# A fused top-k attention and MLP kernel: which tiles VectorE turns, when the weights' second half is converted, and the order of some small steps

## The chip, the core and the metric

The kernel runs on one core of one Trainium2 chip. The metric is the device time of the one launch in microseconds (us). Before the change the median of three runs is 1632.91 us (1632.14 to 1634.82).

## The reference, cut to what matters

```
scores = 1/8 * q @ k^T                      # 8 batches, 8 heads, 576 x 576, head size 64, float32
keep the 32 largest of each row, softmax over them, attn @ v
x  = heads side by side                     # (8, 576, 512)
xn = (x - mean) / sqrt(var + 1e-6) * g_ln
out = x + relu(xn @ w_ch1) @ w_ch2          # 512 -> 2048 -> 512
```

q, k and v are float32. The weights and `g_ln` arrive as 64-bit floats, and the kernel makes 32-bit floats of them from their two 32-bit words.

## The kernel before, in words

**Units, groups, jobs.** A job is one batch and one pair of heads with two or three of the query tiles 0, 1, 2, 3 (128 rows) and 4 (the rest, 64 rows). A unit is one query tile of a job: for a whole tile two score tiles of 128 x 576, one per head; for the rest one tile that holds both heads. There are 68 jobs and 160 units. Batch 0 has the jobs [0,1], then [2,3], then [4], each for four pairs of heads; batch 1 has [0,1] and [2,3,4]; from batch 2 on it is [0,1,4] and [2,3].

**One loop, written out by hand.** `for n in range(END)` emits step n, and nothing is scheduled afterwards: on each engine the instructions run in the order of the code, and wait for each other by semaphores. Step n works on several units at once:

- TensorE makes the scores of unit n+2 (`scores`, L395) and ScalarE copies them out of PSUM (L376).
- VectorE finds the 32nd largest value of each row of unit n in four rounds (`select(u, 0..3)`, L438, L424, L430), and at the step's end takes the maximum and the minimum of the two halves of the next unit (`halve`, L416 and L417). The tile `hi` that `halve` writes has two buffers.
- For unit n-1 (`mk`): `watch` on GpSimd (L457) notes a difference of 2 columns, by which the kernel finds out at its end whether the shortened search was enough; `prepare` on ScalarE (L450, L451) scales threshold and maximum in place; `mask` is an activation on ScalarE (L486) and a subtraction on GpSimd (L489), and `weigh` the exponential on ScalarE (L497).
- For unit n-2 the weights `e` are turned, so that keys lie on partitions, into the tile `pt` (one buffer). This is done in one of two ways. Way one (`turn`): eight TensorE transposes through PSUM (L555) and two ScalarE copies of 128 x 512 (L567). Way two (`move`): two VectorE transposes of 32 x 32 blocks (L528) into the unit's own score tile `sc` (five buffers), then one DMA of 512 KB to HBM (L543), and in step n+3 of the unit four DMAs of 128 KB back into `pt` (L538, `bring`). The last 128 columns of both heads are turned on TensorE in both ways (L584, copied by L585). Way two is taken where `u.moved` is set.
- For a group whose last unit is `lag` steps back: `values` (attention times v, L609 and L616), `take_values` (L624), `place` (transpose L651, scale L628), which fills the rows x of the MLP. `lag` is 2 at first, 4 where the next job's first unit is moved, 3 elsewhere.

**The weights** come in 32 pieces, 16 of `w_ch1` and 16 of `w_ch2`. `batches` says which pieces are split in which step: four ahead of step 0, then 1 or 2 each step for steps 0 to 7 (`w_ch1`), 2 each in steps 8 to 15 (`w_ch2`). A piece is fetched by SP one step ahead (L147, into the pool `x`); `split` is three activations on ScalarE (L163, L164, L167) and, for `w_ch1`, a fourth that multiplies by `g_ln` (L169), and one clamp on GpSimd (L170); `shift` is one VectorE instruction (L173) a step later; `join` is two GpSimd instructions (L179, L181). In steps below `LAZY` = 7 the joins stand at the step's end, later in its middle. `CONVERTING` is the last step with pieces, plus 2.

**The MLP** runs in 18 blocks of 256 rows. `give` adds a block's matmuls to `todo` when its rows are placed; `fill`, called about eight times a step, takes from it as many as the step's `share` allows. The share is even over the steps up to the next block. The first block (`gives_first`, step 9) is the only one whose rows are handed over within the step (`quick`).

**SP** issues all DMAs (ScalarE those of the first two jobs' q), in the order of the code.

The function `compute` with its loop, `split`, `prepare`, `watch`, `settle_watch`, `tell` and `turn` are those that the change touches.

Of the kernel before, what the change touches and what calls it, by code (L numbers as in the profile page):

```python
# [10 lines left out]
ALU = mybir.AluOpType  # L11
# [8 lines left out]
STEEP = 2.0**90  # L20
# [9 lines left out]
def compute(  # L30
# [12 lines left out]
    nc = tc.nc  # L43
    P = nc.NUM_PARTITIONS
# [46 lines left out]
    def const(shape, name):  # L91
        return consts.tile(shape, FP32, tag=name, name=name)
# [5 lines left out]
    def turned():  # L98
        return brief("tp")
# [5 lines left out]
    ends = const([P, P], "ends")  # L105
    nc.gpsimd.memset(ends[:], 0.0)
    if doubt is not None:
        watched = const([P, 34], "watched")
        nc.gpsimd.memset(watched[:], -1.0)
    ident = const([P, P], "ident")  # L110
    make_identity(nc, ident[:])
# [10 lines left out]
    class Piece:  # L122
# [26 lines left out]
        def split(self):  # L149
            i = self.i  # L150
            high = self.raw[:, :, 1].bitcast(FP32)
            if i < NF:
                self.size = hpool.tile([P, DM], U32, tag="h", name="size")[:]
                self.low = wt_rows[:, i % 8]
                homes = ((opool, "o"), (opool, "o"), (rpool, "r"), (rpool, "r"), (xtpool, "xT"))
            else:
                self.size = wt_rows[:, 2 * i % 8].bitcast(U32)
                self.low = wt_rows[:, (2 * i + 1) % 8]
                homes = ((opool, "o"), (opool, "o"), (rpool, "r"))
            pl, tag = homes[i % len(homes)]  # L160
            self.sign = pl.tile([P, DM], FP32, tag=tag, name="sign")
            size_f = self.size.bitcast(FP32)
            nc.scalar.activation(size_f, high, AF.Abs)  # L163
            nc.scalar.activation(  # L164
                self.low, self.raw[:, :, 0], AF.Copy, bias=2.0, scale=2.0**-51
            )
            nc.scalar.activation(self.sign[:], high, AF.Sign)  # L167
            if self.i < NF:
                nc.scalar.mul(self.sign[:], self.sign[:], gcol[:, self.c : self.c + 1])  # L169
            nc.gpsimd.tensor_scalar(size_f, size_f, HIGH_MAX, HIGH_MIN, ALU.min, ALU.max)  # L170

        def shift(self):
            nc.vector.tensor_scalar(  # L173
# [22 lines left out]

    batches = {}
    queue = list(pieces)
    for n in range(-1, NF):
        count = 4 if n < 0 else 1 + (n + 1) % 2 if n < NF // 2 else 2  # L200
        batches[n], queue = queue[:count], queue[count:]
    assert not queue

# [2 lines left out]
    def weights(n, phase):  # L206

        now, before = batches.get(n, []), batches.get(n - 1, [])  # L210
        if phase == 0:
            for x in batches.get(n + 1, []):
                x.fetch()
            for x in now[0::2]:
                x.split()
        elif phase == 1:
            for x in before:
                x.join()
            for x in now[1::2]:
                x.split()  # L220
# [149 lines left out]
    def scores(u):  # L370

        u.sc = scpool.tile([P, 2, S], FP32, tag="sc", name="sc")
        made = [score_half(u, s) for s in range(2)]
        for t in range(len(u.tiles)):
            for s in range(2):
                nc.scalar.copy(  # L376
                    u.sc[:, t, s * HALF : (s + 1) * HALF], made[s][t][:, 0:HALF]
                )
# [67 lines left out]
    def prepare(u):  # L446

        nt = len(u.tiles)
        u.bias, u.edge = u.top[:, 0:nt, 0], u.thr[:, 0:nt, 7]
        nc.scalar.mul(u.edge, u.edge, STEEP)  # L450
        nc.scalar.mul(u.bias, u.bias, -scale)  # L451

    def watch(u):

        nt = len(u.tiles)
        c = 1 + 2 * (u.i % 16)
        nc.gpsimd.tensor_tensor(  # L457
            watched[:, c : c + nt], u.hi[:, 0:nt, HALF + 7], u.thr[:, 0:nt, 7], ALU.subtract
        )
        if u.i % 16 == 15 or u.i == N - 1:  # L460
            u.ends_watch = True

    def settle_watch():

        for out, first, op in ((0, 0, ALU.max), (33, 1, ALU.min)):
            nc.vector.tensor_reduce(
                watched[:, out : out + 1], watched[:, first : first + 33],
                mybir.AxisListType.X, op,
            )

    def tell():

        w = hpool.tile([P, J * P], FP32, tag="h", name="tell")
        nc.gpsimd.memset(w[:], 0.0)
        nc.vector.tensor_scalar(w[:, 1:2], watched[:, 33:34], -1.0e38, None, ALU.is_le)
        nc.vector.tensor_scalar(w[:, 0:1], watched[:, 0:1], 0.0, None, ALU.is_ge)
        nc.vector.tensor_tensor(w[:, 0:1], w[:, 0:1], w[:, 1:2], ALU.max)
        ps = brief("tell")
        nc.tensor.transpose(ps[:, 0:P], w[:, 0:P], ident[:])
        nc.vector.tensor_reduce(w[0:1, P : P + 1], ps[0:1, 0:P], mybir.AxisListType.X, ALU.max)  # L480
        nc.vector.tensor_copy(doubt, w[0:1, P : P + 1])
# [64 lines left out]
    def turn(u):  # L546

        g = u.group
        i0 = place_of(u)
        q0 = i0 * 32  # L550

        def part(t):
            ps = turned()
            for c in range(J):
                nc.tensor.transpose(  # L555
                    ps[:, c * P : (c + 1) * P], u.e[:, t, c * P + t * R : (c + 1) * P + t * R],
                    ident[:],
                )
            if u.rest:
                both = ps[:].rearrange("p (c h n) -> p h c n", h=2, n=R)  # L560
                for h in range(2):
                    nc.scalar.copy(
                        g.blocks[:, h, i0 : i0 + R // 32],
                        both[:, h].rearrange("p c (i n) -> p i c n", n=32),
                    )
            else:
                nc.scalar.copy(  # L567
                    g.blocks[:, t, i0 : i0 + P // 32],
                    ps[:].rearrange("p (c i n) -> p i c n", c=J, n=32),
                )  # L570

        def last():
            ps = turned()
            if u.rest:
                nc.tensor.transpose(ps[0:R, 0:P], u.e[:, 0, JP:S], ident[:])
                nc.tensor.transpose(ps[:, P : 2 * P], u.e[:, 0, JP - R : S], ident[:])
                for h in range(2):
                    nc.scalar.copy(
                        g.pt[h * R : (h + 1) * R, 2 * J, q0 : q0 + R],
                        ps[h * R : (h + 1) * R, h * (P + R) : h * (P + R) + R],  # L580
                    )
            else:
                ends = u.e[:].rearrange("p t n -> p (t n)")[:, JP : JP + P]
                nc.tensor.transpose(ps[:, 0:P], ends, ident[:])  # L584
                nc.scalar.copy(g.pt[:, 2 * J, q0 : q0 + P], ps[:, 0:P])  # L585

        heads = () if u.moved else range(len(u.tiles))
        return [lambda t=t: part(t) for t in heads] + [last]

    xs, xps, rs, oTr, dr = {}, {}, {}, {}, {}  # L590

# [30 lines left out]
    def take_values(g):  # L622
        g.oT = otpool.tile([P, GQ], FP32, tag="oT", name="oT")
        nc.scalar.copy(g.oT[:, 0 : g.nq], g.av[:, 0 : g.nq])  # L624
# [405 lines left out]
    CONVERTING = max(n for n in batches if batches[n]) + 2  # L1030
    EARLY = jobs[NHP].first

    for u in units[jobs[5 * NHP].first :]:
        u.moved = not u.rest and u is not u.group.units[-1]


    for j, after_j in zip(jobs, jobs[1:] + [None]):
# [43 lines left out]
    def at(i):  # L1081
        return units[i] if 0 <= i < N else None
# [10 lines left out]
    def due(n):  # L1093

        return units[n + 2 : n + 3]
# [87 lines left out]
    for n in range(END):  # L1185
# [15 lines left out]

        moved = ex is not None and ex.moved

        if n:
            for x in due(n):
                scores(x)
        if g:
            values(g)
        if n in brings:
            brings.pop(n)()  # L1210
            turn(at(n - 3))[-1]()
        if quick:
            take_values(g)
        if u:
            select(u, 0)
        if quick:
# [8 lines left out]
        if n in keeps:  # L1225
            keep_heads(keeps[n])
        if doubt is not None and at(n - 2) and at(n - 2).ends_watch:
            settle_watch()
            if n == N + 1:
                tell()  # L1230
        if mk and doubt is not None:
            watch(mk)
        if early:
            prepare(ex)
            for t in range(2):
                mask(ex, t)
            if n < gives_first - 1:
                weights(n, 0)
            for t in range(2):
                weigh(ex, t)  # L1240
        if not early or n == gives_first - 1:
            weights(n, 0)
        fill()
        if mk and not early:
# [4 lines left out]
            mask(mk, 1)  # L1249
        if g and not quick:  # L1250
            take_values(g)
        if parts:
            parts[0]()
        if ex and ex.rest:
# [25 lines left out]
        fill()  # L1280
        if n in ends_due:
            fill_ends(ends_due.pop(n))
        if g and not quick:
            place(g)
        if late:
            place_rest(late.job.b, late.job.hp)
        fill(1 if g or late else 0)
        if mk and mk.i >= EARLY:
            weigh(mk, 0)
        fill()  # L1290
        if len(parts) > 2:
            parts[1]()
# [20 lines left out]
        fill()  # L1313
        if u:
            select(u, 3)
        if nxt:
            halve(nxt)
        if n < LAZY:
# [76 lines left out]
```

## Time and profile before

| what | value |
|---|---|
| runs, median of three | 1632.91 us |
| the profiled execution's own time | 1631.76 us |
| its span | 1629.8 us |
| granted TensorE clock, mean | 0.969 |
| TensorE busy | 1499.9 us |
| VectorE busy | 1348.7 us |
| ScalarE busy | 1108.6 us |
| GpSimd busy | 1029.1 us |
| DMA traffic | 211.49 MB, 45.2% of 16 engines' span on SP's queue |
| VectorE transposes of `e` (L528) | 144 instructions for 72 units |
| TensorE transposes of `e` (L555) | 576 instructions |
| last unit's `halve` starts | 1468.2 us after the start |

Line numbers are those of the kernel before. PE is TensorE, PEld its weight loads, DVE VectorE, ACT ScalarE, POOL GpSimd; a "q" behind a name is that engine's queue. Busy time is the union of an engine's instructions. An engine is idle before an instruction while it waits for another engine; the profile names the one that came last. A step of the loop is read on VectorE, from one `halve` (L416) to the next.

### The profile page before, as it was taken

To read this page: it belongs to the slowest core of one execution; us is meant where nothing else is said; L and a number is where in the kernel's file an instruction comes from. 1 tells how busy PE (TensorE), PEld (TensorE's weight loads), DVE (VectorE), ACT (ScalarE), POOL (GpSimd) and SP (SyncE) were. 2 spreads that over 40 slices of the span, in tenths; PEclk is the share of its full clock that TensorE was granted. 3 is DMA by queue.
4 is the path that set the end of the run, shared out by engine and by line. 5 is a ranking of instruction groups with operands and counts; after the bars stand their busy time and mean duration, and the time that the engine had idled before them with its cause. 6 is when DMAs were issued, how large, how long until landed. Compare 5 with 4: busy or idle time off the path is not lost.

```text
span 1629.8 us, 27190 instructions
## 1 busy us (share of the span) xinstructions
PE 1499.9 (92%) x7898; PEld 1131.1 (69%) x7898; DVE 1348.7 (83%) x3939; ACT 1108.6 (68%) x3032; POOL 1029.1 (63%) x1473
## 2 busy tenths in 40 slices
PE   2556889899999999999999999999999999999997
PEld 1334646577767677777777777777777777778886
DVE  6866679698999999999999998998899999992000
ACT  6885767678777676777666867677667776764311
POOL 4775875865666676767765747465657666656344
PEclk9867899999999999999999999999999999999999
DMA  8432335312365456545564465546554455432211
GB/s 216 134 99 82 111 80 118 118 57 68 85 167 180 120 148 166 162 145 142 152 189 133 137 152 172 163 116 175 146 171 149 127 155 159 155 98 85 66 39 54
DMA packets 355685, 211.49 MB, mean 130 GB/s; under 512 B 247492, under 2 KB 327880, under 8 KB 355528
## 3 DMA queue, kind: packets, MB, share of 16 engines
q1 hardware_dynamic: 350792, 209.08, 45.2%
q8 instruction: 65, 1.06, 0.3%
q10 hardware_dynamic: 4736, 0.59, 0.2%
q14 instruction: 92, 0.75, 0.2%
HBM read 145.62 MB, written 63.96 MB: 129 GB/s over the span
## 4 chain that ended last, share of the span: by engine, by line
PE 64%; POOL 15%; ACT 12%; DVE 7%; issue 1%; DMA 1%; ACTq 0%; SPq 0%; POOLq 0%; DVEq 0%
PE hps L754 23%; PE ops L911 19%; PE scps L395 8%; POOL e L489 6%; PE av L609 5%; ACT e L486 3%; PE tp L555 3%; DVE m L438 2%; DVE hi L424 2%; PE av L616 2%; ACT sc L376 2%; POOL h L847 1%; ACT e L497 1%; POOL w L181 1%; PE xo L651 1%
## 5 line engine op out<-in xcount | busy, mean ns | idle before, releaser
L489 POOL TENSOR_TENSOR e<-e,sc 128x576 f32<-128x576 f32 x288 | 423.1, 1486 | 441.1 <-ACT e L486 434.0
L754 PE MATMUL hps<-xT,w 128*128 128x256 f32 x2304 | 546.2, 384 | 7.3 <-ACT xT L716 7.3
L754 PEld LDWEIGHTS hps<-xT,w 128*128 128x128 f32 x2304 | 425.0, 192 | 74.1 <-issue 11.5
L438 DVE MAX8 m<-hi 128x8 f32<-128x296 f32 (+1 forms) x1152 | 471.2, 444 | 0.2
L424 DVE MATCH_REPLACE8 hi<-m,hi 128x288 f32<-128x288 f32 (+1 forms) x864 | 377.7, 442 | 0.0
L911 PE MATMUL ops<-w,h 128*128 128x256 f32 x1360 | 322.3, 383 | 1.4 <-POOL h L847 1.4
L911 PEld LDWEIGHTS ops<-w,h 128*128 128x128 f32 x1360 | 251.3, 192 | 40.1 <-issue 5.8
L376 ACT COPY sc<-scps 128x288 f32<-128x288 f32 x576 | 199.1, 407 | 99.3 <-PE scps L395 77.7
L497 ACT ACTIVATE e<-e,m 128x576 f32<-128x576 f32 x288 | 224.8, 781 | 59.5 <-POOL e L489 58.0
L486 ACT ACTIVATE e<-sc,m 128x576 f32<-128x576 f32 x288 | 212.4, 769 | 0.0
L416 DVE TENSOR_TENSOR hi<-sc 128x576 f32<-128x576 f32 (+1 forms) x160 | 135.4, 846 | 59.7 <-POOL watched L457 55.3
L609 PE MATMUL av<-pt,vb 128*64 128x256 f32 (+2 forms) x1088 | 147.2, 412 | 5.9 <-ACT pt L567 4.8
L417 DVE TENSOR_TENSOR lo<-sc 128x576 f32<-128x576 f32 (+1 forms) x160 | 144.1, 901 | 0.0
L555 PE MATMUL tp<-ident,e 128*128 128x128 f32 x576 | 94.0, 291 | 47.0 <-ACT e L497 47.0
L395 PE MATMUL scps<-kT,late_qT 64*128 64x288 f32 (+3 forms) x832 | 129.2, 419 | 8.6 <-ACT pt L567 6.0
L777 ACT ACTIVATE h<-hps 128x512 f32<-128x512 f32 x144 | 85.2, 592 | 66.7 <-PE hps L754 65.7
L911 PE MATMUL ops<-wt,s 128*128 128x256 f32 x544 | 129.3, 381 | 0.0
L555 PEld LDWEIGHTS tp<-ident,e 128*128 128x128 f32 x576 | 76.8, 150 | 69.7 <-ACT e L497 52.3
L528 DVE STREAM_TRANSPOSE sc<-e 128x512 f32<-128x512 f32 x144 | 94.3, 687 | 33.4 <-POOL h L847 16.7
L609 PEld LDWEIGHTS av<-pt,vb 128*64 128x64 f32 x1088 | 72.8, 141 | 67.2 <-issue 15.5
L430 DVE MAX8 hi<-lo 128x8 f32<-128x288 f32 x288 | 117.7, 444 | 0.0
L395 PEld LDWEIGHTS scps<-kT,late_qT 64*128 64x128 f32 (+1 forms) x832 | 72.3, 171 | 61.8 <-issue 18.7
(104 smaller groups left out, 1887.4 us busy)
## 6 DMA issues: line engine op xcount, KB each, us to landing
turned<-sc SPq DMA_DIRECT2D x72, 512.0 KB, 2.9
pt<-turned SPq DMA_DIRECT2D x288, 128.0 KB, 2.7
w<-forms SPq DMA_DIRECT2D x136, 256.0 KB, 3.9
vb<-in_v_dram SPq DMA_DIRECT2D x68, 288.0 KB, 3.9
raw<-in_moe_w_ch_dram SPq DMA_DIRECT2D x32, 512.0 KB, 3.5
kT<-kept SPq DMA_DIRECT2D x36, 288.0 KB, 3.5
kin<-in_k_dram SPq DMA_DIRECT2D x128, 72.0 KB, 2.8
kept<-kT SPq DMA_DIRECT2D x32, 288.0 KB, 3.0
```

The lines of the kernel that those rows point to most:

```text
L376: nc.scalar.copy(u.sc[:, t, s * HALF : (s + 1) * HALF], made[s][t][:, 0:HALF])
L395: nc.tensor.matmul(ps[i * R : i * R + ql, o : o + width], qT[r, q0 : q0 + ql], kT[r, k0 : k0 + width], start=True, stop=True,)
L417: nc.vector.tensor_tensor(lo, a, b, ALU.min)
L424: nc.vector.match_replace(x, m[:, t, :], x, LOWEST)
L438: nc.vector.max(m[:, t, :], u.hi[:, t, 0:width])
L486: nc.scalar.activation(u.e[:, t], u.sc[:, t], AF.Relu, bias=u.edge[:, t : t + 1], scale=-STEEP)
L489: nc.gpsimd.tensor_tensor(u.e[:, t], u.e[:, t], u.sc[:, t], ALU.subtract)
L497: nc.scalar.activation(u.e[:, t], u.e[:, t], AF.Exp, bias=u.bias[:, t : t + 1], scale=-scale, accum_out=g.den[:, col : col + 1],)
L555: nc.tensor.transpose(ps[:, c * P : (c + 1) * P], u.e[:, t, c * P + t * R : (c + 1) * P + t * R], ident[:],)
L609: nc.tensor.matmul(av[h * D : (h + 1) * D, 0 : g.nq], vb[:, h * (J + 1) + c, :], g.blocks[:, h, 0 : g.nq // 32, c, :], start=(c == 0), sto ...
L754: nc.tensor.matmul(ps[0][:, side * N : (side + 1) * N], w1[:, c, f * P : (f + 1) * P], self.xT[:, c, 0:N], start=(c == 0), stop=(c == NC - 1),
L911: nc.tensor.matmul(bank[name][:, 0:Q], a(j), rhs, start=first and j == 0, stop=(j == G - 1), skip_group_check=not first,)
```

## The change

- **More units are moved.** `u.moved` was set from batch 2 on for whole tiles that are not the last of their group. It is now set from unit 8 (`EARLY`) on for every whole tile that is not its job's last, and for a job's last one too where the next job begins with a whole tile. In the built program VectorE has 236 transposes of `e` where it had 144, TensorE 368 transposes of `e` (heads and ends together) where it had 736, ScalarE 20 copies of 128 x 512 where it had 112, and SP 118 and 472 DMAs for the moves where it had 72 and 288. So 118 units are moved where 72 were; of the 46 new ones 7 are moved in steps 10 to 16, 15 in steps 22 to 39, 23 in steps 40 to 158 and 1 in step 159.
- **The weights' second half pauses.** Steps 8 and 9 split nothing; `w_ch2` is split in steps 10 to 17. `CONVERTING` becomes 19.
- **The factor g_ln** is multiplied on GpSimd (16 instructions of 128 x 512) and no longer on ScalarE; the clamp is emitted ahead of it.
- **The note** `watch` is emitted at the end of its unit's own step, and not at the start of the next. Its store is doubled, and `prepare` writes the scaled threshold to another column, so that it need not wait for the note.
- **Order.** Up to step 9 `values` (and at step 9 `take_values`) come ahead of `scores`. The ends of a moved unit are transposed where they were, but copied later, after the masks. `place` and `place_rest` come after a fill and the first `weigh`. At step 8 the weights stand between the masks and `weigh` as in the steps before it.

```diff
             nc.scalar.activation(size_f, high, AF.Abs)
+            nc.gpsimd.tensor_scalar(size_f, size_f, HIGH_MAX, HIGH_MIN, ALU.min, ALU.max)
...
             nc.scalar.activation(self.sign[:], high, AF.Sign)
             if self.i < NF:
-                nc.scalar.mul(self.sign[:], self.sign[:], gcol[:, self.c : self.c + 1])
-            nc.gpsimd.tensor_scalar(size_f, size_f, HIGH_MAX, HIGH_MIN, ALU.min, ALU.max)
+                nc.gpsimd.tensor_scalar(
+                    self.sign[:], self.sign[:], gcol[:, self.c : self.c + 1], 1.0,
+                    ALU.mult, ALU.mult,
+                )
...
-    for n in range(-1, NF):
-        count = 4 if n < 0 else 1 + (n + 1) % 2 if n < NF // 2 else 2
+    for n in range(-1, NF + 2):
+        count = 4 if n < 0 else 1 + (n + 1) % 2 if n < NF // 2 else 0 if n < NF // 2 + 2 else 2
...
-        u.bias, u.edge = u.top[:, 0:nt, 0], u.thr[:, 0:nt, 7]
-        nc.scalar.mul(u.edge, u.edge, STEEP)
+        u.bias, u.edge = u.top[:, 0:nt, 0], u.thr[:, 0:nt, 6]
+        nc.scalar.mul(u.edge, u.thr[:, 0:nt, 7], STEEP)
...
-    for u in units[jobs[5 * NHP].first :]:
-        u.moved = not u.rest and u is not u.group.units[-1]
+    for j, nj in zip(jobs, jobs[1:] + [None]):
+        for u in units[max(j.first, EARLY) : j.last + 1]:
+            u.moved = not u.rest and (
+                u.i < j.last or nj is not None and not units[nj.first].rest
+            )
...
-        if n:
-            for x in due(n):
-                scores(x)
-        if g:
+        late_ends = None
+        ahead = due(n) if n else []
+        if g and n <= gives_first:
+            values(g)
+        if quick:
+            take_values(g)
+        for x in ahead:
+            scores(x)
+        if g and n > gives_first:
             values(g)
         if n in brings:
             brings.pop(n)()
-            turn(at(n - 3))[-1]()
-        if quick:
-            take_values(g)
+            late_ends = turn_ends(at(n - 3))
...
-        if mk and doubt is not None:
-            watch(mk)
...
+        if late_ends:
+            late_ends()
...
+        fill(1 if g or late else 0)
+        if mk and mk.i >= EARLY:
+            weigh(mk, 0)
         if g and not quick:
             place(g)
         if late:
             place_rest(late.job.b, late.job.hp)
-        fill(1 if g or late else 0)
-        if mk and mk.i >= EARLY:
-            weigh(mk, 0)
...
         if u:
             select(u, 3)
+            if doubt is not None:
+                watch(u)
```

`turn_ends` is the former last part of `turn`, with the transposes and the copy separated; `watched`, `settle_watch` and `tell` follow the doubled store.

More of the change, by code (lines that the diff above doesn't have):

```diff
@@ L107, in compute @@
     if doubt is not None:
-        watched = const([P, 34], "watched")
+        watched = const([P, 2, 34], "watched")
         nc.gpsimd.memset(watched[:], -1.0)
@@ L455, in watch @@
         nt = len(u.tiles)
-        c = 1 + 2 * (u.i % 16)
+        half, c = u.i // 16 % 2, 1 + 2 * (u.i % 16)
         nc.gpsimd.tensor_tensor(
-            watched[:, c : c + nt], u.hi[:, 0:nt, HALF + 7], u.thr[:, 0:nt, 7], ALU.subtract
+            watched[:, half, c : c + nt], u.hi[:, 0:nt, HALF + 7], u.thr[:, 0:nt, 7], ALU.subtract
         )
@@ L461, in watch, with settle_watch @@
             u.ends_watch = True
-    def settle_watch():
+            u.half = half
+    def settle_watch(half):
         for out, first, op in ((0, 0, ALU.max), (33, 1, ALU.min)):
             nc.vector.tensor_reduce(
-                watched[:, out : out + 1], watched[:, first : first + 33],
+                watched[:, half, out : out + 1], watched[:, half, first : first + 33],
                 mybir.AxisListType.X, op,
@@ L474, in tell @@
         nc.gpsimd.memset(w[:], 0.0)
-        nc.vector.tensor_scalar(w[:, 1:2], watched[:, 33:34], -1.0e38, None, ALU.is_le)
-        nc.vector.tensor_scalar(w[:, 0:1], watched[:, 0:1], 0.0, None, ALU.is_ge)
-        nc.vector.tensor_tensor(w[:, 0:1], w[:, 0:1], w[:, 1:2], ALU.max)
+        nc.vector.tensor_scalar(w[:, 2:4], watched[:, :, 33], -1.0e38, None, ALU.is_le)
+        nc.vector.tensor_scalar(w[:, 4:6], watched[:, :, 0], 0.0, None, ALU.is_ge)
+        nc.vector.tensor_reduce(w[:, 0:1], w[:, 2:6], mybir.AxisListType.X, ALU.max)
         ps = brief("tell")
@@ L572, in last, with turn_ends, copy @@
         def last():
-            ps = turned()
+            turn_ends(u)()
+        heads = () if u.moved else range(len(u.tiles))
+        return [lambda t=t: part(t) for t in heads] + [last]
+    def turn_ends(u):
+        q0 = place_of(u) * 32
+        g = u.group
+        ps = turned()
+        if u.rest:
+            nc.tensor.transpose(ps[0:R, 0:P], u.e[:, 0, JP:S], ident[:])
+            nc.tensor.transpose(ps[:, P : 2 * P], u.e[:, 0, JP - R : S], ident[:])
+        else:
+            ends_e = u.e[:].rearrange("p t n -> p (t n)")[:, JP : JP + P]
+            nc.tensor.transpose(ps[:, 0:P], ends_e, ident[:])
+        def copy():
             if u.rest:
-                nc.tensor.transpose(ps[0:R, 0:P], u.e[:, 0, JP:S], ident[:])
-                nc.tensor.transpose(ps[:, P : 2 * P], u.e[:, 0, JP - R : S], ident[:])
                 for h in range(2):
@@ L582, in last @@
             else:
-                ends = u.e[:].rearrange("p t n -> p (t n)")[:, JP : JP + P]
-                nc.tensor.transpose(ps[:, 0:P], ends, ident[:])
                 nc.scalar.copy(g.pt[:, 2 * J, q0 : q0 + P], ps[:, 0:P])
-        heads = () if u.moved else range(len(u.tiles))
-        return [lambda t=t: part(t) for t in heads] + [last]
+        return copy
     xs, xps, rs, oTr, dr = {}, {}, {}, {}, {}
@@ L1227, in compute @@
         if doubt is not None and at(n - 2) and at(n - 2).ends_watch:
-            settle_watch()
+            settle_watch(at(n - 2).half)
             if n == N + 1:
                 tell()
-        if mk and doubt is not None:
-            watch(mk)
         if early:
@@ L1236, in compute @@
                 mask(ex, t)
-            if n < gives_first - 1:
-                weights(n, 0)
+            weights(n, 0)
             for t in range(2):
                 weigh(ex, t)
-        if not early or n == gives_first - 1:
+        if not early:
             weights(n, 0)
```

## The prediction

> **What bounds the kernel now.** I read the busy time in five stretches first, cut at the starts of VectorE's steps 9, 19 (235 us), 40 and 159; columns: stretch, length, busy time and instructions of PE, PEld, DVE, ACT, POOL, granted clock, DMA share, GB/s.
>
> ```profile
> 0.00:111.00 111.00, 50.57 (x212) 31.63 (x212) 83.16 (x247) 89.12 (x206) 73.48 (x83) 0.86 0.58 157
> 111.00:235.00 124.00, 94.04 (x410) 61.20 (x411) 81.70 (x239) 88.02 (x218) 88.78 (x91) 0.82 0.31 95
> 235.00:418.00 183.00, 174.99 (x982) 123.57 (x983) 152.84 (x481) 135.91 (x388) 115.97 (x166) 0.97 0.33 86
> 418.00:1468.00 1050.00, 1028.19 (x5553) 783.78 (x5550) 1018.61 (x2934) 752.30 (x2121) 676.52 (x997) 1.00 0.53 149
> 1468.00:1630.00 162.00, 152.07 (x745) 130.91 (x743) 12.41 (x40) 43.27 (x102) 74.34 (x137) 0.99 0.20 61
> ```
>
> No engine fills the first two stretches: steps there hang on chains between engines. In the third TensorE is at 96% and VectorE at 84%. In the fourth both are at 97 to 98%. The fifth is the last blocks' matmuls; VectorE has next to nothing left. Up to 1468 VectorE is idle for 27.8 + 42.3 + 30.2 + 31.4 = 131.7 us. Where, the waits of VectorE and ScalarE tell (total us, times, longest):
>
> ```profile
> DVE hi L416 <- POOL watched L457: 55.3, 27, 7.1
> DVE wt L173 <- POOL wt L170: 28.8, 6, 8.4
> ACT pt L585 <- PE tp L584: 76.2, 50, 4.5
> ACT m L450 <- POOL watched L457: 54.8, 35, 5.1
> ACT sign L167 <- POOL w L181: 18.1, 5, 4.8
> ```
>
> The first is VectorE's `halve` waiting for its buffer until GpSimd has noted; 10.5 us of it lie in the first stretch, 2.9 in the second, 24.7 in the third, 17.2 in the fourth. The second lies in steps 11 to 16, where the weights' second half is converted. Then the prices, from the groups (busy us, mean ns, idle before):
>
> ```profile
> L528 DVE STREAM_TRANSPOSE sc<-e 128x512 f32<-128x512 f32 x144 | 94.3, 687 | 33.4 <-POOL h L847 16.7 <-ACT e L497 16.1 <-POOL e L489 0.6
> L555 PE MATMUL tp<-ident,e 128*128 128x128 f32 x576 | 94.0, 291 | 47.0 <-ACT e L497 47.0
> L567 ACT COPY pt<-tp 128x512 f32<-128x512 f32 x112 | 65.4, 584 | 17.2 <-PE tp L555 16.7
> L169 ACT ACTIVATE sign<-sign,gcol 128x512 f32<-128x512 f32 x16 | 11.6, 722 | 0.5
> L170 POOL TENSOR_SCALAR size<-size 128x512 f32<-128x512 f32 x16 | 11.2, 698 | 19.8 <-ACT size L163 19.8
> ```
>
> Last, step 9 in order of time (start, duration, idle before): scores go ahead of the first block's values, and VectorE waits for the rows.
>
> ```profile
> 117.28 2.46 PE L395 MATMUL scps<-kT,late_qT 64*128 64x288 f32 x6
> 120.57 1.33 PE L395 MATMUL scps<-kT,late_qT 64*128 64x288 f32 x2 [0.83 <-ACT pt L567]
> 121.82 3.68 PE L609 MATMUL av<-pt,vb 128*64 128x256 f32 x16
> 128.04 0.70 DVE L679 BATCH_NORM_STATS2 st<-x 128x6 f32<-128x512 f32 x1 [9.35 <-ACT x L628]
> ```
>
> **One more moved unit** costs VectorE two L528 at 94.3/144 = 0.655 us: 1.31 us. It saves TensorE eight L555 at 94.0/576 = 0.163 us: 1.3 us, and ScalarE two L567: 1.17 us. SP issues five DMAs more. For 46 units: 60.3 us more on VectorE, 60.1 less on TensorE, 53.7 less on ScalarE, 47 MB more traffic. What counts is where VectorE has room. The Trainium skill (VectorE: DVE Perf Modes, "Rules for kernel authors") speaks against this: a 128 x 128 transpose belongs on TensorE if PSUM will do as its destination. By that rule alone the 60.3 us would be a plain loss, an estimate of 1693 us; the rows above disagree so far as VectorE idles beside a TensorE at 96%.
>
> **Stretch 1, to step 8: -7 us.** From step 3 on ScalarE sets the pace: its L450 starts at 45.7 us and, six steps later, at 111.1, so 10.9 us a step, while VectorE has 8.1 to 9.5 of work. ScalarE loses L169: seven pieces in steps 3 to 8, 7 x 0.72 = 5.1 us. At the start L450 waits 5.07 us for a note that stands behind eight joins; these still stand before the subtraction, so I count 2 of it. The new 16 factors on GpSimd cost about what the clamp costs undisturbed, 0.615 us, 9.8 in all; GpSimd waits 1.6 to 3.2 us a step for masks there, and that covers them. If it doesn't, they delay the note and the subtraction: +5. If all of `halve`'s waits go: -10.5.
>
> **Stretch 2, steps 9 to 18: -11 us.** Values ahead of scores bring the rows earlier by 121.82 - 117.28 = 4.5 us, and step 8 starts 1.5 us sooner without `halve`'s wait: -6. VectorE's wait of 9.35 us covers no more than that. The pause moves eight steps of pieces by two, with all their instructions and 16 fetches; it removes none, so its value is only that ScalarE and GpSimd enter them without arrears. In steps 12 to 15 (52.3 us, 13.1 each) the loop is: first join, sign of the next piece, exponentials, copies, next split, masks, subtraction, join; VectorE waits about 4.4 us a step beside it, so seven moves at 1.31 (9.2 us) are covered there, and ScalarE's loop loses one or two L567 each. I take -5 for these, between -29 (all 28.8 us of L173's wait gone) and +9 (the moves paid in full). Later weights delay the first block's second product by two steps; TensorE has room for it (76% busy).
>
> **Stretch 3, steps 19 to 39: -3 us.** 15 moves: VectorE 152.8 + 19.7 = 172.5; TensorE 175 - 19.5 = 155.5. So VectorE becomes the bound here. Of its 30.2 us of waits, steps 25 to 27 hold 12.9, where the note stood behind four form-making instructions of 1.27 us; it is now ahead of them. I leave 7.5: 180 instead of 183. Ends: 172.5 (-11) and 202.7 (+20, no wait shrinks).
>
> **Stretch 4, steps 40 to 158: +12 us.** 23 moves: VectorE 1018.6 + 30.1 = 1048.7, which is the whole stretch of before. TensorE falls to 998. Its relief ends some of VectorE's 31.4 us of waits, and ScalarE gets free of L585 (65.8 us here, for the copy now stands behind the masks) and of L450's 31.7. But `watch` keeps its place on GpSimd behind the same subtractions. I leave 13 of 31.4: 1062. Ends: 1049 (-1) and 1080 (+30).
>
> **Queues.** On SP each new unit puts a send behind the fetches, which wait for ScalarE (L147 behind L167: 103.1 us in 21 waits, 4.9 each), and four reads that wait for `values` to free `pt` (L538 behind L616: 195.2 us in 41). Behind the send waits only the score buffer's next use, in the step after; a 512 KB send lands in 2.9 us. A group's last unit now arrives one step ahead of its values, not two: 1.7 us of issue and 2.8 of landing in a step of 8.7. No time counted; without that cover one landing, about 4.5 us, a group in the weights' steps. The copy `late_ends` and `place` only move behind work of their own engine.
>
> **Tail: 0.** The work behind the last unit is the same but for one moved unit; its VectorE time lies beside 152 us of TensorE.
>
> **Sum:** -7 - 11 - 3 + 12 = -9 on a span of 1629.8: 1620.8. Around the span lie 1631.76 - 1629.8 = 2.0 us, and the median is 1.15 above that run: 1624.
>
> On the port: with L179 at 134.07 us taking 1.77 us, its usual 1.27, VectorE's L417 took 1.81 instead of 0.75. The Trainium skill (SBUF — State Buffer, "Who interferes with whom") says a VectorE instruction with two SBUF inputs and a GpSimd one exclude each other for a whole instruction; by it the factors could hold VectorE for up to 16 x 0.615 = 9.8 us, an estimate, and the sum would be 1634. I keep 1624: the factors run in the first stretch alone, where VectorE isn't the bound.
>
> **Rivals.**
> - *VectorE pays in full from step 19 on* (slower side). Its 38 new moves cost 49.8 us, and its waits there, 30.2 + 31.4, stay because GpSimd's queue and not TensorE ends them: with stretches 1 and 2 at -18 that is +32, 1665; with 18 us of waits gone 1647. For it: 41.9 of the 61.6 us are the wait for the note, behind GpSimd. Against: GpSimd itself waits 434 us for ScalarE's masks, and ScalarE is relieved. It decides when over 45 x 1.31 = 59 of the 131.7 us of idle can't be filled, that is, when more than 72.7 remain.
> - *The weights' steps run at VectorE's pace.* 81.7 + 9.2 = 90.9 us of work, about 8 of waiting in step 9 and 4 elsewhere: stretch 2 takes 103 and not 113, so 1614. For it: ScalarE's copies leave the loop. Against: GpSimd alone has 10 us a step.
> - *SP is late.* The send held by 4.9 us and passed on to ScalarE's copies in the seven units of stretch 2: up to +34, more likely a quarter of it, which takes the gain away: 1633. For it: L147's waits. Against: ScalarE waited only 4.0 us for sends so far.
> - That it doesn't do what it says: 118 units and not 117 are moved, which changes nothing; and where no joins or forms lie between, the note keeps its place.
>
> **Chances.** Forecast, 1614 to 1633: 0.46, of which 0.08 lie within 0.2%. Weights' steps: 0.19. SP: 0.08, half within, half slower. VectorE in full: 0.27. A measurement here can tell 0.2%, 3.3 us. Faster 0.38 + 0.19 = 0.57; same 0.08 + 0.04 = 0.12; slower 0.04 + 0.27 = 0.31. The forecast's own range, 1612 to 1634, lets each stretch miss by a fifth of its bounds; the range that leaves out no more than 2 in 10 runs from 1602, below the second case, to 1648, the first rival's middle.
>
> **What would show it.** Stretch 4 on VectorE at 1049 us or more busy and under 15 idle; L416's wait for the note under 25 in all; L173's wait still about 20; step 9 at 17 us; L450's wait near none; TensorE idle in the fourth stretch. If VectorE's idle time before the last unit stays over 80 us, the forecast is wrong; if it falls under 55, the second rival is right.

## The result, and the profile after

The changed kernel takes 1661.6 us (median of four runs, 1657.9 to 1663.9) against 1633.6 us for the kernel before in the same session (1632.1 to 1634.8): a ratio of 1.017, 95% interval 1.0149 to 1.0191. The forecast said 1624 us, and slower at most 1648. The profiled execution has a span of 1660.4 us, 30.6 more than before.

Line numbers of the changed kernel differ a little: `halve` is now L419 (maximum) and L420 (minimum), VectorE's transposition of `e` is L532, the note is L460, the factor is L170 on GpSimd.

First the five stretches, cut again at the starts of VectorE's steps 9, 19, 40 and 159. Columns as before: stretch, length, busy time and instructions of PE, PEld, DVE, ACT, POOL, granted clock, DMA share, GB/s.

```profile
0.00:116.00 116.00, 53.83 (x212) 33.78 (x212) 88.51 (x247) 79.10 (x193) 91.19 (x98) 0.81 0.54 145
116.00:243.00 127.00, 95.22 (x383) 58.53 (x385) 93.74 (x253) 82.58 (x207) 86.14 (x89) 0.84 0.52 154
243.00:434.00 191.00, 164.05 (x860) 118.91 (x858) 183.83 (x511) 123.22 (x362) 130.26 (x174) 0.92 0.55 158
434.00:1497.00 1063.00, 1017.56 (x5334) 770.63 (x5331) 1055.81 (x2982) 715.58 (x2063) 694.20 (x993) 0.98 0.59 171
1497.00:1660.00 163.00, 153.64 (x749) 132.25 (x747) 13.63 (x41) 43.50 (x102) 74.35 (x137) 0.99 0.22 68
```

From one cut to the next the kernel is 5, 3, 8, 13 and 2 us longer. VectorE is now the fullest engine of the third and the fourth stretch (96% and 99%), and TensorE has room there. Then the groups of VectorE that matter (busy us, mean ns, idle before), and the factor's group:

```profile
L420 DVE TENSOR_TENSOR lo<-sc 128x576 f32<-128x576 f32 (+1 forms) x160 | 169.7, 1060 | 0.0
L532 DVE STREAM_TRANSPOSE sc<-e 128x512 f32<-128x512 f32 x236 | 153.2, 685 | 28.6 <-POOL h L863 14.1 <-ACT e L501 8.8 <-POOL s L857 5.8
L419 DVE TENSOR_TENSOR hi<-sc 128x576 f32<-128x576 f32 (+1 forms) x160 | 144.3, 902 | 11.7 <-POOL watched L460 7.5 <-ACT sc L379 4.2
L170 POOL TENSOR_SCALAR sign<-sign,gcol 128x512 f32<-128x512 f32 x16 | 14.0, 873 | 2.5 <-ACT sign L168 1.4
```

In the kernel before, the two halving lines were these:

```profile
L417 DVE TENSOR_TENSOR lo<-sc 128x576 f32<-128x576 f32 (+1 forms) x160 | 144.1, 901 | 0.0
L416 DVE TENSOR_TENSOR hi<-sc 128x576 f32<-128x576 f32 (+1 forms) x160 | 135.4, 846 | 59.7 <-POOL watched L457 55.3 <-ACT sc L376 4.1
```

The wait for the note fell from 55.3 to 7.5 us, as hoped. But the same 320 instructions became 34.5 us longer (279.5 to 314.0). The other waits of before are gone or moved (total us, times, longest):

```profile
ACT e L501 <- POOL e L493: 126.8, 141, 7.2
ACT sc L379 <- DMA turned<-sc: 87.2, 33, 5.6
...
ACT pt L597 <- PE tp L589: 6.6, 10, 1.2
```

and in the kernel before:

```profile
ACT e L497 <- POOL e L489: 58.0, 97, 2.3
ACT sc L376 <- DMA turned<-sc: 4.0, 3, 2.1
```

ScalarE no longer waits for the ends (76.2 us before, 6.6 now) nor for the note; it waits for GpSimd's masks instead (58.0 before, 126.8 now) and for the sends of transposed tiles (4.0 before, 87.2 now). Last, the chain that ended last, of the changed kernel and of the kernel before: VectorE has 30% of it (7% before), transfers 6% (1% before).

```profile
PE 47%; DVE 30%; POOL 9%; ACT 7%; DMA 6%; issue 2%; SPq 0%; ACTq 0%; POOLq 0%; DVEq 0%
PE 64%; POOL 15%; ACT 12%; DVE 7%; issue 1%; DMA 1%; ACTq 0%; SPq 0%; POOLq 0%; DVEq 0%
```

### The profile page after: what moved, and what is told of

The parts are those of the page before. It is cut to its first block, busy times and chain, and to the rows that moved or that the text cites. A ratio compares the mean times of both kernels' runs of the same rounds, so it can differ in the third digit from the quotient of the medians.

```text
span 1660.4 us, 26850 instructions
## 1 busy us (share of the span) xinstructions
PE 1484.3 (89%) x7530; PEld 1114.1 (67%) x7530; DVE 1435.5 (86%) x4031; ACT 1044.0 (63%) x2924; POOL 1076.1 (65%) x1489
## 2 busy tenths in 40 slices
DMA packets 388807, 259.74 MB, mean 156 GB/s; under 512 B 251172, under 2 KB 355112, under 8 KB 388648
## 4 chain that ended last, share of the span: by engine, by line
PE 47%; DVE 30%; POOL 9%; ACT 7%; DMA 6%; issue 2%; SPq 0%; ACTq 0%; POOLq 0%; DVEq 0%
PE hps L770 17%; PE ops L927 15%; DVE m L441 9%; DVE hi L427 7%; PE scps L398 6%; PE av L625 4%; DVE sc L532 4%; DMA turned<-sc 3%; POOL e L493 3%; DVE lo L420 3%; DVE hi L419 3%; DVE hi L433 2%; DMA pt<-turned 2%; ACT sc L379 1%; PE av L632 1%
## 5 line engine op out<-in xcount | busy, mean ns | idle before, releaser
L770 PE MATMUL hps<-xT,w 128*128 128x256 f32 x2304 | 535.8, 385 | 0.7 <-ACT xT L732 0.7
L770 PEld LDWEIGHTS hps<-xT,w 128*128 128x128 f32 x2304 | 434.9, 194 | 65.0 <-issue 7.0
L441 DVE MAX8 m<-hi 128x8 f32<-128x296 f32 (+1 forms) x1152 | 470.0, 443 | 0.1
L379 ACT COPY sc<-scps 128x288 f32<-128x288 f32 x576 | 196.6, 408 | 197.6 <-DMA turned<-sc 87.2
L501 ACT ACTIVATE e<-e,m 128x576 f32<-128x576 f32 x288 | 223.9, 778 | 128.2 <-POOL e L493 126.8
L927 PEld LDWEIGHTS ops<-w,h 128*128 128x128 f32 x1360 | 257.4, 195 | 37.4 <-issue 1.9
L532 DVE STREAM_TRANSPOSE sc<-e 128x512 f32<-128x512 f32 x236 | 153.2, 685 | 28.6 <-POOL h L863 14.1
L420 DVE TENSOR_TENSOR lo<-sc 128x576 f32<-128x576 f32 (+1 forms) x160 | 169.7, 1060 | 0.0
L419 DVE TENSOR_TENSOR hi<-sc 128x576 f32<-128x576 f32 (+1 forms) x160 | 144.3, 902 | 11.7 <-POOL watched L460 7.5
L398 PE MATMUL scps<-kT,late_qT 64*128 64x288 f32 (+3 forms) x832 | 124.7, 414 | 2.1 <-ACT x L644 1.4
L625 PEld LDWEIGHTS av<-pt,vb 128*64 128x64 f32 x1088 | 77.8, 143 | 68.9 <-issue 13.1
L927 PEld LDWEIGHTS ops<-wt,s 128*128 128x128 f32 x544 | 106.1, 201 | 16.4 <-issue 1.9
L398 PE MATMUL scps<-kT,qT 64*128 64x288 f32 x512 | 93.0, 462 | 20.1 <-DVE qT L328 11.8
```

What stands on the lines that cost most here:

```text
L379: nc.scalar.copy(u.sc[:, t, s * HALF : (s + 1) * HALF], made[s][t][:, 0:HALF])
L398: nc.tensor.matmul(ps[i * R : i * R + ql, o : o + width], qT[r, q0 : q0 + ql], kT[r, k0 : k0 + width], start=True, stop=True,)
L420: nc.vector.tensor_tensor(lo, a, b, ALU.min)
L441: nc.vector.max(m[:, t, :], u.hi[:, t, 0:width])
L501: nc.scalar.activation(u.e[:, t], u.e[:, t], AF.Exp, bias=u.bias[:, t : t + 1], scale=-scale, accum_out=g.den[:, col : col + 1],)
L532: nc.vector.transpose(blocks.rearrange("p (j t c n) -> p j t c n", j=ni, t=2, c=J)[:, :, t], u.e[:, t, t * R : t * R + JP].rearrange("p (c ...
```

## The experiments

Twelve kernels ran, each beside the kernel before on the same chip. One theory runs through them: transpositions moved to VectorE are paid there, because its idle time does not last. It was sharpened by what each run showed.

**1. The old set of moved units in the changed kernel (e1), and the new set alone in the kernel before (e2).**

```
-    for j, nj in zip(jobs, jobs[1:] + [None]):
-        for u in units[max(j.first, EARLY) : j.last + 1]:
-            u.moved = not u.rest and (
-                u.i < j.last or nj is not None and not units[nj.first].rest
-            )
+    for u in units[jobs[5 * NHP].first :]:
+        u.moved = not u.rest and u is not u.group.units[-1]
```

The lines above are e1; e2 is the same edit the other way round, in the kernel before.

> The changed kernel with the set of moved units of before (72, not 118); all else as changed. Theory 1 (the transposes are paid on VectorE, which was full from step 40 on and nearly full from 19): 46 x 1.31 = 60 us leave VectorE, 60 come back to TensorE; the time falls from 1662 to 1620-1632 us, and halve's wait for the note stays short. Theory 2 (what costs is halve running into GpSimd's instructions since the note and the factor moved): VectorE's busy time for the two halving lines stays near the 314 us that it has after the change (280 before), and the time stays above before, at 1640-1655. If neither, and SP or the DMA traffic was to blame, it falls below 1620.

> The kernel before with the new set of moved units alone (118). Theory 1: 1650-1665, as slow as the changed kernel; VectorE's idle time before the last unit falls below 90 us from 131.7, for the moves fill it. Theory 2: 1635-1645, for halve still starts behind the note and the halving lines stay near 280 us. A rival, that the moves hit SP behind the weights' fetches in steps 10 to 16, shows as a longer stretch of steps 9 to 18 (over 135 us where before has 124).

Measured: e1 1623.7 us, ratio 0.9936 (0.9915 to 0.9958); e2 1667.2 us, ratio 1.0208 (1.0176 to 1.024). Steps 9 to 18 of e2 take 125 us, not over 135. So the moves are the whole loss, 34 us on the kernel before (2 us over the range of the first theory) and 38 on the rest of the change, and that rest alone is a gain of 10. The second theory's times missed, but the halving lines are long in both kernels: 316.1 us in e2, where it expected 280, and 322.6 in e1. So slower halving does not by itself mean a slower kernel; e1 has it and is faster than the kernel before.

**2. The factor back on ScalarE (e3), the note back at the start of the next step (e4), in the changed kernel.**

```
-                nc.gpsimd.tensor_scalar(
-                    self.sign[:], self.sign[:], gcol[:, self.c : self.c + 1], 1.0,
-                    ALU.mult, ALU.mult,
-                )
+                nc.scalar.mul(self.sign[:], self.sign[:], gcol[:, self.c : self.c + 1])
```

```
+        if mk and doubt is not None:
+            watch(mk)
         if early:
             prepare(ex)
...
             select(u, 3)
-            if doubt is not None:
-                watch(u)
```

> The changed kernel with g_ln's factor back on ScalarE. If the factor on GpSimd costs the first steps what the trace suggests (GpSimd busy 91 us to step 8 where before has 73; steps 0 to 8 take 105.0 us and not 99.8), this takes 5 to 10 us off: 1652-1657. If ScalarE is what bounds those steps, as the prediction had it, it adds 5: 1667.

> The changed kernel with the note again at the start of the next step; the threshold's own column stays, so ScalarE doesn't wait for the note. Theory 2: the halving lines fall back towards 280 us busy, from 314, and halve's wait for the note returns (some 30-50 us); if the two cancel, the time stays within 4 us of 1662: the wait was only exchanged for slower instructions. If the note's new place is itself the loss, the time falls by 10 us or more. If the note's new place was a gain, it rises.

Measured: e3 1661.4 us (ratio 1.0176, 1.0152 to 1.0199), e4 1664.2 us (1.0189, 1.016 to 1.0217). Neither time is told apart from the changed kernel's. For e4 that was expected, but not in the expected way: `halve`'s wait for the note came back to 20.7 us only, not 30 to 50, and its two lines stayed at 315.5 us instead of falling towards 280. So the trade of this wait for slower halving is not shown by the note's place. e3 missed both its numbers: the factors on GpSimd take 14.0 us, and where they run makes no difference.

**3. Where the moves cost: the new set below unit 40 only (e6), from unit 40 on only (e7).** Behind the new rule, e6 and e7 put the old one back for the other units:

```
+    for u in units[40:]:
+        u.moved = u.i >= jobs[5 * NHP].first and not u.rest and u is not u.group.units[-1]
```

(e7: `units[:40]`.)

> The changed kernel with its own set of moved units only below unit 40 (22 new units); from unit 40 on the set of before. Theory 1 (each new unit is paid on VectorE where it stands, in its 1.31 us and in slower two-input instructions beside GpSimd; the costs add): the changed kernel reaches step 40 17 us later than the run with the old set (434 against 417), so 1623.7 + 17 = 1641 us, within 5. Rival (the early moves leave arrears behind that last through the long stretch): 1655 to 1663. Rival (in the first 40 steps VectorE has room, and only the long stretch pays): 1622 to 1628.

> The changed kernel with its own set of moved units only from unit 40 on (24 new units); below it the set of before. Theory 1 (the costs add): steps 40 to 158 took 1063 us with the new set against 1044 with the old, and what is behind them 1.7 more, so 1623.7 + 20.7 = 1644 us, within 5. Rival (arrears of the early moves): 1622 to 1630. Rival (only the long stretch pays): 1657 to 1663.

Measured: e6 1637.0 us (ratio 1.0026, 1.0017 to 1.0036), e7 1645.6 us (1.0078, 1.0056 to 1.0099). Against e1 that is +13 and +22, together 35 of the 38: the costs add. The 22 new moves of e6 are 29 us of VectorE's time at 1.31 us each and cost 13; the 24 of e7 are 31 us and cost 22. So neither part covers its moves in full, and neither carries the whole loss.

**4. The slow instructions taken away (e8 in the changed kernel, e9 in the kernel before).** VectorE's halving reads two inputs. In one place of the changed kernel, the timeline (start, duration, idle before) shows it beside GpSimd's forming of the weights:

```profile
292.70 0.20 POOL L460 TENSOR_TENSOR watched<-hi,m 128x2 f32<-128x2 f32 x1
292.85 1.27 POOL L981 TENSOR_TENSOR wt<-w 128x512 f32<-128x512 f32 x1
292.94 1.80 DVE L419 TENSOR_TENSOR hi<-sc 128x576 f32<-128x576 f32 x1 [0.31 <-POOL watched L460]
294.20 1.66 POOL L982 TENSOR_TENSOR wt<-w,wt 128x512 f32<-128x512 f32 x1
294.66 1.82 DVE L420 TENSOR_TENSOR lo<-sc 128x576 f32<-128x576 f32 x1
295.94 1.67 POOL L983 TENSOR_TENSOR form<-wt,w 128x512 f32<-128x512 f32 x1
```

In the kernel before the note stood behind these forms, and `halve` waited for it and then ran alone:

```profile
289.13 1.26 POOL L968 TENSOR_TENSOR form<-w,wt 128x512 f32<-128x512 f32 x1
290.35 0.20 POOL L457 TENSOR_TENSOR watched<-hi,m 128x2 f32<-128x2 f32 x1
290.58 0.76 DVE L416 TENSOR_TENSOR hi<-sc 128x576 f32<-128x576 f32 x1 [3.52 <-POOL watched L457]
291.26 0.75 DVE L417 TENSOR_TENSOR lo<-sc 128x576 f32<-128x576 f32 x1
```

So in this place a wait of 3.52 us became 0.31 and two instructions 2.11 us longer, and two of GpSimd's 0.4 us longer each. The edit puts instructions with one input in the place of those with two; e8 and e9 leave out the maximum and the minimum:

```
-        nc.vector.tensor_tensor(hi, a, b, ALU.max)
-        nc.vector.tensor_tensor(lo, a, b, ALU.min)
+        for t in range(nt):
+            nc.vector.transpose(hi[:, t], a[:, t])
+        for t in range(nt):
+            nc.vector.transpose(lo[:, t], b[:, t])
```

> The changed kernel with halve's maximum and minimum left out: in their place each of the two halves of the scores is written to the same buffer by a VectorE instruction with one input (a transposition of 128x288, two a half). The selection then works on other numbers; the thresholds of tell are set so that they never apply. Theory 1 (the new moves cost more than VectorE's idle time because halve's two-input instructions run slower beside GpSimd): halve's two lines took 314 us; 640 transpositions at 0.38 to 0.42 us are 243 to 269, so VectorE, the bound from step 19 on, loses 45 to 70 us: 1592 to 1617 us, and no later than 6 us behind the same edit made to the kernel before. Rival (the collisions don't matter; the transposed units are the whole cost): 20 us or more behind the same edit made to the kernel before.

> The kernel before with the same edit: halve's maximum and minimum left out, transpositions with one input in their place. Theory 1: halve's two lines took 279 us, so VectorE loses 10 to 36 us, of which idle time takes a part: 1605 to 1628 us; the changed kernel with this edit stands at most 6 us behind it or ahead of it. Rival (collisions don't matter): 1625 to 1635 and the changed kernel 20 us or more behind it.

Measured: e8 1623.3 us (ratio 0.994, 0.9922 to 0.9958), e9 1615.5 us (0.9897, 0.988 to 0.9915). The changed kernel gains 38 us by the edit, the kernel before 18, and of the 28.1 us between them 7.7 are left. That is 2 us more than the theory allowed and far from the rival's 20; e8 itself is 6 us above its range, although VectorE lost more work (78.2 us; 576 transpositions run there, not the 640 expected). The same place of e8's timeline:

```profile
281.87 0.20 POOL L462 TENSOR_TENSOR watched<-hi,m 128x2 f32<-128x2 f32 x1
282.02 1.27 POOL L983 TENSOR_TENSOR wt<-w 128x512 f32<-128x512 f32 x1
282.10 0.84 DVE L420 STREAM_TRANSPOSE hi<-sc 128x288 f32<-128x288 f32 x2 [1.55 <-POOL watched L462]
282.86 0.80 DVE L422 STREAM_TRANSPOSE lo<-sc 128x288 f32<-128x288 f32 x2
283.37 1.28 POOL L984 TENSOR_TENSOR wt<-w,wt 128x512 f32<-128x512 f32 x1
```

The two engines run side by side here at their undisturbed durations.

One reading stays open. The edit also takes work from VectorE, 40.9 us in the kernel before, and leaves it more idle time there (153.0 us instead of 131.7). So a part of the 20 us can come from this room for the moves, and not from the missing slow-down. The fourth stretch speaks against much of that: there the change lowers VectorE's idle time by 24 us in either form, and its cost falls from 12.9 to 1.4 us, about the 12.1 us by which halving had grown. In the third stretch the cost hardly falls, from 7.7 to 6.4 us.

**5. The pause undone: in the changed kernel (e5), and with the old set of moves (e11); the note back with the old set (e10).** The edit of e5 and e11 (e10 has that of e4):

```
-    for n in range(-1, NF + 2):
-        count = 4 if n < 0 else 1 + (n + 1) % 2 if n < NF // 2 else 0 if n < NF // 2 + 2 else 2
+    for n in range(-1, NF):
+        count = 4 if n < 0 else 1 + (n + 1) % 2 if n < NF // 2 else 2
```

> The changed kernel with the order of the weights' pieces of before (two pieces in each of steps 8 and 9, no pause). Theory 1 (the new moves are the cost; the pause only shifts pieces): within 5 us of the changed kernel, 1657 to 1667. Rival (the pause is a cost: later weights hold back the first block's second product and with it the steps from 19 on): 1645 to 1655. Rival (the pause is a gain that keeps ScalarE and GpSimd free of arrears): 1668 to 1680, with steps 9 to 18 over 131 us (126.7 in the changed kernel).

> The kernel with the changed code and the old set of moved units, and with the note back at the start of the next step. Theory 1 (the early note only exchanges halve's wait for slower two-input instructions): within 4 us of 1623.7, VectorE idle in steps 19 to 158 some 20 us over the 15 of the early note and its excess over undisturbed durations as much lower. Rival (the early note is what makes the run with the old set faster than the kernel before): 1629 to 1636.

> The kernel with the changed code and the old set of moved units, and with the order of the weights' pieces of before (no pause). Theory 1 (the pause is worth little): within 4 us of 1623.7. Rival (the pause is what makes the run with the old set faster than the kernel before): 1629 to 1636. If it costs: under 1619.

Measured: e5 1659.3 us (ratio 1.0156, 1.0123 to 1.019), e11 1620.1 us (0.993, 0.9908 to 0.9951), e10 1624.6 us (0.9945, 0.9928 to 0.9963). The pause is worth nothing, perhaps 2 to 4 us the wrong way; the intervals overlap. e10's time is that of e1, as the theory said, but its other number missed: VectorE's idle time in steps 19 to 158 is 15.2 us, not 20 more than e1's 15.1, and its halving lines take 320.8 us against e1's 322.6. With the old note the wait for it comes to 19.3 us and not 55.3, so something else of the change had already shortened it.

**6. The rest alone (e12): the old moves, pieces, factor and note; the threshold's own column, the values ahead of scores, the late copy of the ends and the later placing stay.** Its edit is those of e1, e3, e4 and e5 together.

> What is left of the change without its moves, its pause, its factor and its early note: the old set of moved units, the old order of the pieces, the factor on ScalarE and the note at the start of the next step; the threshold's own column, the values ahead of scores, the late copy of the ends and the later placing stay. Theory 1 (the 5 to 6 us that the changed kernel loses up to step 8 come from GpSimd, which took factors and notes; the gain over the kernel before comes from the rest): step 9 starts at 109 to 112 us instead of 116, and 1614 to 1619 us in all. Rival (VectorE's waits and slower instructions are exchanged for one another in the first stretch too): step 9 at 114 to 117 and 1618 to 1623. Rival (factor and note bring the gain): 1626 or more.

Measured: 1621.6 us, ratio 0.9923 (0.991 to 0.9937). Step 9 starts at 116.4 us: the rival had it right. The gain comes from these small parts, which of them was not tried, and the first stretch's loss of 5 us comes with them too, not with the factor or the note.

What the runs say together stands in one table (us; VectorE's transpositions of `e`, its two halving lines, and its idle time before the last unit):

| kernel | time | VectorE busy | transpositions | halving | idle |
|---|---|---|---|---|---|
| before | 1633.6 | 1348.7 | 94.3 | 279.5 | 131.7 |
| rest alone (e12) | 1621.6 | 1387.6 | 93.2 | 319.5 | 83.0 |
| moves alone (e2) | 1667.2 | 1437.6 | 152.9 | 316.1 | 79.0 |
| changed kernel | 1661.6 | 1435.5 | 153.2 | 314.0 | 75.1 |
| before, one input (e9) | 1615.5 | 1307.8 | 95.5 | 236.0 | 153.0 |
| changed, one input (e8) | 1623.3 | 1357.3 | 154.8 | 235.5 | 115.0 |

In the two-input form each of the three kernels with a part of the change or all of it has 49 to 57 us less idle time on VectorE than the kernel before, and 35 to 40 us more of halving. The rest alone took 48.7 us of idle time, and 40.0 us came back as slower halving: a gain of 10 in the span. The groups of e12:

```profile
L417 DVE TENSOR_TENSOR lo<-sc 128x576 f32<-128x576 f32 (+1 forms) x160 | 165.2, 1033 | 0.0
L416 DVE TENSOR_TENSOR hi<-sc 128x576 f32<-128x576 f32 (+1 forms) x160 | 154.3, 964 | 24.3 <-POOL watched L457 19.2 <-ACT sc L376 4.9
```

After that VectorE had no room left from step 19 on (16 us idle), and the moves' 60 us brought 40 us of time (e12 against the changed kernel; the pause, the factor and the note differ too, and e3, e4, e5 and e11 found each of them worth little or nothing). Of the kernels that keep the maximum and the minimum none beat e11 and e12, which stand 0.7 to 0.8% below the kernel before.

## Why the prediction was wrong

**The first step that failed is the paragraph on the port.** It showed one halving instruction at 1.81 us instead of 0.75 beside GpSimd, asked only what the new factors could do to VectorE ("up to 9.8 us"), and then said: "I keep 1624: the factors run in the first stretch alone, where VectorE isn't the bound." The disturbance was not tied to the factors. As `halve` waited less, it ran more often beside GpSimd's joins, forms and masks, and its two instructions grew. The sum credited the waits and put this growth at nothing: halving became 34.5 us longer.

**The terms of the first two stretches failed too**, and only in part by the port. The forecast had -7 and -11 us there, and they measured +5.4 and +2.7; halving grew by 8.3 us in them, and the two terms missed by 26. The table gives the stretches in us, forecast and measured; the last column but one is the change in the one-input form (the profiled execution of e9 is 3 us under its median).

| stretch | forecast | change | rest alone (e12) | moves alone (e2) | e8 less e9 | halving longer by |
|---|---|---|---|---|---|---|
| 1 | -7 | +5.4 | +5.4 | +0.2 | +3.6 | 4.4 |
| 2 | -11 | +2.7 | -1.3 | +1.3 | -1.4 | 3.9 |
| 3 | -3 | +7.7 | -3.9 | +7.0 | +6.4 | 14.0 |
| 4 | +12 | +12.9 | -10.2 | +26.4 | +1.4 | 12.1 |
| tail | 0 | +1.9 | 0.0 | +2.1 | +1.6 | 0.0 |

In VectorE's account the forecast's first four stretches are 59 us more work and 68 less idle time; measured were 85.2 more and 56.6 less. So the work was put 26 us too low, and the growth of halving is more than that. The idle time was to fall by 27 us in the first two stretches and fell by 9; in the next two it fell by 6 more than foretold.

What the growth cost in time is an estimate. The one-input edit took 78.2 us of work from VectorE in the changed kernel and 38 us of time, and 40.9 and 18 in the kernel before, a little under a half. By that share the 34.5 us are worth some 15 to 17 us of the 38 by which the forecast missed. Even with the growth gone (e8 against e9) the change costs 7.7 us instead of gaining.

The Trainium skill (SBUF — State Buffer, "Who interferes with whom") had the rule: a VectorE instruction with two SBUF inputs contends with a GpSimd one that reads SBUF, and one with at most one such input does not, outside the two-port modes that the page sets apart. Both halves agree with the rows of experiment 4 (1.80 and 1.82 us against 0.84 and 0.80 for the same elements). What the prediction missed was to apply it to `halve` in every stretch.

**Price of a move.** 236 - 144 = 92 transpositions more cost 58.9 us, against 60.3 foretold, and the traffic grew by 48 MB (211.49 to 259.74), against 47. The rule weighed against them, that such a transposition belongs on TensorE (the Trainium skill, VectorE: DVE Perf Modes, "Rules for kernel authors"), would have made it 1693 us as a plain loss; e2, the moves alone, is at 1667.2, on the rule's side though not as far.

**Stretch 1: -7 foretold, +5.4 measured.** The step that failed is "ScalarE sets the pace". ScalarE lost 10 us of work there, and it gained nothing; e3 gave it 9 us back (88.8 us busy), and the stretch was not longer for it (114.5 against 116.4 us). L450's wait went away as foretold. GpSimd became the fullest engine (73 to 91 us busy), but e12, which has GpSimd back at 74 us in steps 0 to 8, is no faster there. What holds the first stretch stays open.

**Stretch 2: -11 foretold, +2.7 measured.** The values did come earlier: they start 6.1 us into step 9, not 10.8, and the step takes 18.8 us, not 22.7 (17 foretold).

```profile
122.47 4.09 PE L625 MATMUL av<-pt,vb 128*64 128x256 f32 x16
126.50 0.70 PE L632 MATMUL av<-pt,ends 128*128 128x256 f32 x2
127.12 1.24 PE L398 MATMUL scps<-kT,late_qT 64*128 64x288 f32 x8
```

The other 5 us, for moves "covered" beside the weights' loop, failed: the wait that was to cover them stayed (28.8 to 25.5 us), and steps 9 to 18 take 126.7 us with the new moves against 120.3 with the old (e1), and 124.2 against 119.7 without the pause (e5, e11).

**Stretch 3: -3 foretold, +8 measured.** The idle time left was foretold at 7.5 and is 7.2; VectorE's work was foretold at 172.5 and is 183.8. In this account that difference of 11 is the whole error of the stretch. But in the one-input form, where halving doesn't grow, the stretch is still 6.4 us longer, with 14.4 us of idle time on VectorE; what holds it then was not found out. VectorE's instructions there stand 19.0 us in all above their undisturbed durations (5.3 before), counting by what each exceeds the 20th percentile of its operation, tile and shape.

**Stretch 4: +12 foretold, +13 measured.** Right in size, but by luck, with two errors against each other: VectorE 1055.8 us busy, not 1048.7, and idle 7.2, not 13. TensorE's relief was too large as well: 1017.6 us busy there, not 998, and over the whole span 15.6 us less, not 60.1, at a mean granted clock of 0.948 instead of 0.969.

**Tail: 0 foretold, +1.9 measured.** Not looked into further.

**The signs.** Those on VectorE's idle time, on the note (7.5 us, under 25), on L450 and on TensorE's idle time in the fourth stretch all came true, and even the bound of 80 us on VectorE's idle time before the last unit (75.1) raised no alarm; step 9 at 17 us did not quite (18.8). They were signs that waits go away; none looked at what the instructions behind the waits would then take.

**The rivals.** "VectorE pays in full from step 19 on" gave 1665 us at its extreme, near the 1661.6 measured, but its mechanism was another: its waits were to stay, and they fell from 61.6 to 14.4 us. Its turning point, more than 72.7 us of idle time left, spoke for it by a hair (75.1). "The weights' steps run at VectorE's pace" did not occur. "SP is late" did occur as a wait, 87.2 us of ScalarE for sends; these sends hold up the scores, and VectorE's `halve` waited for scores for 4.2 us in all (L419 above). From step 19 on VectorE, the fullest engine, idles 14.4 us altogether, so little of it can have reached VectorE there. In e8 the wait is still 61.6 us, and there the whole change costs 7.7. No run took the sends away by themselves. "It doesn't do what it says" falls: 236 transpositions are 118 units.

## What to carry to other kernels

A wait is not free time until it is known what the instruction behind it does when it starts earlier: here, in the rest alone, 40.0 us of slower two-input instructions stand against 48.7 us of idle time removed. Before moving work to an engine that idles, take the mean duration of its two-input groups against their undisturbed minimum, beside the idle time, and debit it. The kernel before already showed it: its two halving lines had means of 846 and 901 ns, and took 0.76 and 0.75 us in the place shown where no GpSimd instruction ran beside them. When a change bundles several edits, run the one that adds work apart from the rest: here the rest was a gain of 12 us under a loss of 40.

## What the runs showed of the hardware

The slow-down runs both ways. With the halving of the changed kernel in one-input form, GpSimd's own groups get shorter at the same work: the additions and subtractions over the hidden layer's parts (L857, L858, L859 and L863) fall from 566, 536, 516 and 520 ns to about 460 each. One of them in the changed kernel:

```profile
L857 POOL TENSOR_TENSOR s<-h 128x128 f32<-128x128 f32 x136 | 76.9, 566 | 4.5 <-ACT h L793 4.4
```

and the same one with one-input halving (e8, whose line numbers are higher by two):

```profile
L859 POOL TENSOR_TENSOR s<-h 128x128 f32<-128x128 f32 x136 | 62.3, 458 | 4.5 <-ACT h L795 4.4
```

In all, GpSimd's busy time falls from 1076.1 to 963.6 us. Two of VectorE's one-input lines hardly change: the transposition of `e` took 685 ns in the changed kernel and 688 in e8, the MAX8 of L441 443 and 439. And TensorE's granted clock in the third stretch was 0.92 in the changed kernel and 0.97 before, though TensorE was busy for less of it (164 of 191 us against 175 of 183).
